# Retention with a gated feed-forward: the order table of the first two batches laid anew, with 25 unread matmuls on zeros among TensorE's first instructions

## The chip, the cores and the metric

One Trainium2 chip, one core of it. The metric is the device time of one execution in microseconds (us), median of several runs. The engines are PE (TensorE), DVE (VectorE), ACT (ScalarE), POOL (GpSimd) and SP, whose queue issues all DMAs of this kernel. Each engine runs its own instructions strictly in program order and waits for others by semaphores.

## The reference

For 8 batches of 8 heads, 576 positions and head width 64:

```python
scores = q @ k.T / sqrt(64)
ret    = scores * D            # D[i, j] = gamma_head ** (i - j) for i >= j, else 0
x      = ret @ v               # heads joined: 576 x 512 per batch
h      = max(x @ w_in, 0)      # 576 x 1024; u = left half, v = right half
v_n    = (v - mean) / sqrt(var + 1e-6)        # over the 512 features
v_s    = w_spatial @ v_n + b_spatial          # mixes the 576 positions
out    = (u * v_s) @ w_out                    # 576 x 512
```

## The kernel before

**Staging.** Matmul operands are float32 split into two rounded parts (`hi`, `lo`), so a product takes three matmuls (hi·hi, hi·lo, lo·hi). The attention runs in chunks of 128 positions (four and a tail of 64 per batch) with a carried state. The weights come from memory as 64-bit floats and are decoded on chip, 128 rows or columns at a time. Batches 0 and 1 use the plain products; batches 2 to 7 use a seven-product scheme on 2 x 2 quarters, whose sums of weight quarters are made once, during the first two batches.

**The order is a table.** Every piece of work is a chain of steps (a Python generator). A table of names says in which order the steps are emitted: each appearance of a name emits the next step of that chain. `ORDER` (656 names) covers batches 0 and 1 and the beginnings of 2 and 3; `STEADY` (249 names) is walked six times, for batches 2 to 7. A step puts instructions on one engine, and the engine keeps the order in which they were emitted. `BANKS` gives, in turn, the PSUM bank (0 to 3) of every step that takes one; a bank is free again when its last reader has run. All instructions are recorded by one helper, so that rows of the profile have one line, L155, and tiles tell them apart.

The names that matter:

- `d.b.c` fetches chunk c of batch b (queries and keys, then the two token-wise parts), `T.b` its tail, `D.k.i` the raw words of weight piece i of kind k (1: right half of `w_in`, 0: left half, 2: `w_out`), `S` the spatial weights, `c.*` constants.
- `w.k.i.xy` decodes a weight piece in seven steps: ACT absolute value; a maximum on engine x (`p` POOL, `v` DVE); three integer steps on DVE, for which a PSUM bank holds the intermediate from the first on until the third has read it; ACT cast to `hi`; on engine y the subtraction that gives `lo`.
- `g.b.c` scores on PE and their mask on DVE; `k`, `q` scale keys and queries; `p.b.c.xy` updates the state (PE, add, decay on x, add on DVE, decay on y); `b.b.c` carries the state and multiplies by the values on PE, then ACT takes `hi` and DVE `lo` of the chunk of x out of PSUM (from batch 2 on ACT alone). `t`, `e` do the same for the tail; the `e` steps leave its `hi` and `lo` in the tile `xt`.
- `v.b.s` is a block of the right half of `h`: four PE steps into a bank, then a chain over ACT and DVE (statistics, normalisation, `hi`, `lo`) that holds the bank to its end; `v.b.4` is the tail block and needs `xt`.
- `U`, `V`, `G`, `P` (batch 0) and `y`, `X` (batch 1) make u, the spatial product, the gate and the split of the gated result; `F.b.t.m` is the output product, copied out by ACT and stored. `F.0.0.1`, the first of them, needs `P.0.0` and `P.0.1`.
- `A.s.n` are the steps that make sums of weight quarters, `R` and `K` the splits and sums of quarters of x for batch 2; `W` are the products of batches 2 to 7. The first, `W.2.0.0.6`, needs both parts of `K.2.6`.

`spin`, which a name `z` calls, is in the kernel before but no table of before has a `z`:

```python
idle = wsp[0][:, 0, :512]              # set to zero by DVE at the start
def spin(name, n):
    ps = bank()
    for i in range(n):
        pe.matmul(ps, idle[:, :P], idle, start=True, stop=True)
```

`idle` is later overwritten by the spatial weights (`s.0`), so `s.0` comes after every `z`.

Of the kernel before, what the change touches and what calls it, by code (L numbers as in the profile page):

```python
# [38 lines left out]


ORDER = """
    D.1.1 w.1.1.vp D.1.0 D.1.3 w.1.1.vp d.0.0 c.k w.1.1.vp D.1.2 c.a w.1.0.vp d.0.0 w.1.3.pp w.1.3.pp w.1.0.vp
# [4 lines left out]
    p.0.1.vv v.0.0 p.0.1.vv k.0.2.p b.0.1 w.0.0.vp b.0.1 q.0.2.p w.0.0.vp g.0.2 b.0.1 w.0.1.pp w.0.1.pp b.0.1
    p.0.2.pp T.0 p.0.1.vv d.0.3 w.0.2.pp p.0.2.pp v.0.0 b.0.1 v.0.0 g.0.2 w.0.1.pp p.0.2.pp w.0.1.pp b.0.2 p.0.2.pp
    b.0.2 c.t w.0.2.pp p.0.2.pp v.0.1 v.0.1 t.0.p t.0.p w.0.1.pp k.0.3.v b.0.2 b.0.2 d.1.0 w.0.2.pp q.0.3.p g.0.3
    t.0.p p.0.3.pp v.0.1 p.0.3.pp v.0.0 v.0.1 p.0.3.pp b.0.2 b.0.2 v.0.2 g.0.3 S d.1.0 p.0.3.pp d.1.1 b.0.3 m  # L50
    w.0.0.vp b.0.3 d.1.1 v.0.1 g.1.0 b.0.3 b.0.3 k.1.0.p w.0.2.pp S v.0.2 v.0.2 d.1.0 v.0.0 D.2.1 q.1.0.p s.0.p
# [34 lines left out]
STEADY = """
    W.a.0.0.6 W.a.0.0.1 W.a.0.0.2.v W.a.0.0.1 W.a.0.0.6 q.b.1.v W.a.0.0.2.v W.a.0.0.5 W.a.0.0.7 W.a.0.0.3
    W.a.0.0.2.v W.a.0.0.7 W.a.0.0.5 W.a.0.0.4 W.a.0.0.5 W.a.0.0.3 W.a.0.0.4 v.a.0.v W.a.0.1.2.p v.a.0.v W.a.0.1.1
    W.a.0.1.7 W.a.0.1.6 k.b.1.p W.a.0.1.1 b.b.0 v.a.2.p W.a.0.1.6 v.a.0.v g.b.1 v.a.0.v T.b v.a.2.p p.b.1.pp b.b.0
    W.a.0.1.2.p b.b.0 g.b.1 d.b.2 b.b.0 W.a.0.1.5 W.a.0.1.2.p W.a.0.1.3 v.a.2.p d.b.2 W.a.0.1.7 p.b.1.pp W.a.0.1.5  # L90
    b.b.0 q.b.2.p d.b.2 W.a.0.1.5 W.a.0.1.4 t.b.p W.a.1.0.1 W.a.0.1.4 p.b.1.pp W.a.0.1.3 k.b.2.p W.a.1.0.6 v.a.3.p
    p.b.1.pp b.b.1 g.b.2 v.a.0.v v.a.1.p v.a.2.p b.b.1 v.a.0.v d.b.3 v.a.3.p W.a.1.0.1 v.a.2.p W.a.1.0.6 p.b.2.vp
    b.b.1 b.b.1 p.b.1.pp g.b.2 d.b.3 W.a.1.0.2.p d.c.0 W.a.1.0.5 b.b.1 p.b.2.vp W.a.1.0.7 k.b.3.p v.a.2.p v.a.4
    W.a.1.0.2.p v.a.4 v.a.1.p W.a.1.0.4 W.a.1.0.2.p W.a.1.0.7 v.a.1.p v.a.3.p v.a.4 d.c.0 p.b.2.vp W.a.1.0.3
    W.a.1.0.5 p.b.2.vp v.a.4 d.b.3 W.a.1.0.5 v.a.4 W.a.1.0.4 W.a.1.1.1 b.b.2 b.b.2 g.b.3 v.a.1.p k.c.0.p W.a.1.0.3
    v.a.4 p.b.3.vp v.a.1.p p.b.2.vp d.c.0 v.a.3.p t.b.p b.b.2 b.b.2 v.a.4 W.a.1.1.6 v.a.1.p v.a.4 v.a.3.p W.a.1.1.1
    q.b.3.p W.a.1.1.2.p p.b.3.vp v.a.4 v.a.3.p W.a.1.1.6 W.a.1.1.7 W.a.1.1.4 v.a.4 W.a.1.1.2.p v.a.4 W.a.1.1.3
    W.a.1.1.7 W.a.1.1.5 W.a.1.1.2.p t.b.p v.a.4 v.a.4 d.c.1 W.a.1.1.5 X.a.1.1 p.b.3.vp W.a.1.1.4 W.a.1.1.5 X.a.0.1
    W.a.1.1.3 X.a.0.1 X.a.0.1 X.a.0.0 b.b.2 p.b.3.vp X.a.0.3 X.a.0.1 b.b.3 X.a.1.1 b.b.3 g.b.3 X.a.1.1 g.c.0 X.a.1.1
    X.a.0.0 p.c.0.pp b.b.3 X.a.0.3 b.b.3 e.b.p X.a.0.3 X.a.0.0 X.a.0.2 X.a.0.3 d.c.1 g.c.0 e.b.p X.a.1.3 e.b.p  # L100
    X.a.1.3 X.a.0.0 R.b.0.0.v X.a.0.2 X.a.0.2 b.b.3 p.c.0.pp p.c.0.pp X.a.1.0 X.a.1.3 X.a.0.2 p.c.0.pp X.a.1.3
    R.b.1.1.p q.c.0.v R.b.0.0.v X.a.1.2 X.a.1.2 d.c.1 K.b.5.pv F.a.0.1 F.a.0.3 X.a.1.0 F.a.0.1 K.b.7.pp F.a.0.2
    X.a.1.0 R.b.1.0.v F.a.0.3 R.b.1.1.p F.a.0.0 X.a.1.2 F.a.0.2 K.b.6.pv F.a.0.2 F.a.0.0 F.a.0.1 p.c.0.pp X.a.1.0
    F.a.0.3 X.a.1.2 F.a.1.1 F.a.1.2 F.a.1.1 F.a.1.3 K.b.6.pv R.b.1.0.v F.a.1.0 F.a.1.2 K.b.5.pv F.a.1.3 K.b.4.pp
    K.b.6.pv F.a.0.0 K.b.7.pp K.b.4.pp F.a.1.0 F.a.1.3 K.b.7.pp F.a.1.2 K.b.4.pp F.a.1.0 F.a.1.1 K.b.5.pv
"""
# [818 lines left out]
```

## Time and profile before

| what | us |
|---|---|
| three runs | 528.2, 528.48, 531.0 (median 528.48) |
| profiled execution, first to last instruction | 526.7 |
| what lies around that span, if that execution was like the median run | 1.8 |

The profile holds no other time for the profiled execution than its span. PE is busy for 95% of it; the granted TensorE clock is 0.996 of full on average. A "busy" PE row is not proof of full speed: rows of neighbouring matmuls overlap, so the distance between starts is the price of one.

### The profile page before, as it was taken

How to read it: one execution, taken by the hardware profiler on the slowest of the kernel's cores; microseconds unless marked ns; L12 is line 12 of the kernel's file. 1: busy time of each engine (PE TensorE's matmuls, PEld its weight loads, DVE VectorE, ACT ScalarE, POOL GpSimd, SP SyncE). 2: the span in 40 equal slices, each digit the busy share in tenths (PEclk: the TensorE clock that was granted, in tenths of full speed). 3: DMA queues.
4: the chain of work that ended last, by engine and by line, in shares of the span. 5: the costliest groups of instructions: out<-in, count | busy, mean ns of one | idle time of the engine just before them, and what ended most of it. 6: DMA issues, size and time to landing. Idle time of an engine off the chain costs nothing.

```text
span 526.7 us, 17043 instructions
## 1 busy us (share of the span) xinstructions
PE 499.3 (95%) x7376; PEld 475.8 (90%) x7376; DVE 353.3 (67%) x803; ACT 222.0 (42%) x502; POOL 236.6 (45%) x216
## 2 busy tenths in 40 slices
PE   0789999999998999999999999999999999999897
PEld 0668998799998999999999999999999999998896
DVE  4998888961536884579654995569745895538640
ACT  4347535562152452444344451445434452444422
POOL 2887769411156720667027740557216750444000
PEclk9999999999998999999999999999999999999999
DMA  8995342403315430163202650155201600020002
GB/s 289 410 321 187 116 157 82 123 18 101 113 59 170 144 105 2 46 197 126 78 2 94 182 168 4 42 157 160 87 2 52 221 11 2 1 91 1 0 1 91
DMA packets 29948, 55.53 MB, mean 105 GB/s; under 512 B 3249, under 2 KB 15793, under 8 KB 29618
## 3 DMA queue, kind: packets, MB, share of 16 engines
q1 hardware_dynamic: 29874, 54.45, 31.4%
q8 instruction: 58, 0.95, 0.7%
q14 instruction: 16, 0.13, 0.1%
HBM read 45.00 MB, written 9.44 MB: 103 GB/s over the span
## 4 chain that ended last, share of the span: by engine, by line
PE 80%; DVE 9%; POOL 3%; issue 3%; DMA 2%; ACT 2%; SPq 0%; ACTq 0%; POOLq 0%; DVEq 0%
PE m L155 69%; PE r L155 11%; DVE u L155 3%; DMA lent_slot<-in_w_in 1%; POOL x L155 1%; DVE sm L155 1%; DMA kn<-in_qkv 1%; POOL u L155 1%; DVE m L155 1%; DVE s L155 1%; DVE vn L155 1%; DVE slot L155 1%; SPq L155 0%; ACT vt L155 0%; DVE dec L155 0%
## 5 line engine op out<-in xcount | busy, mean ns | idle before, releaser
L155 PE MATMUL m<-wsp,vn 128*128 128x288 f32 x768 | 113.5, 297 | 0.4 <-DVE vt L155 0.3
L155 PEld LDWEIGHTS m<-wsp,vn 128*128 128x128 f32 x768 | 105.2, 188 | 2.0 <-DVE vt L155 1.3
L155 PE MATMUL m<-slot,wout 128*128 128x288 f32 x768 | 104.1, 294 | 0.2 <-DVE f L155 0.2
L155 PEld LDWEIGHTS m<-slot,wout 128*128 128x128 f32 x768 | 102.3, 188 | 0.7 <-issue 0.6
L155 PE MATMUL m<-slot,win 128*128 128x288 f32 x480 | 74.2, 299 | 1.8 <-ACT u L155 1.0
L155 DVE TENSOR_TENSOR u<-m,u 128x256 f32<-128x256 f32 (+1 forms) x144 | 59.0, 431 | 24.5 <-ACT u L155 16.5
L155 PEld LDWEIGHTS m<-slot,win 128*128 128x128 f32 x480 | 66.7, 188 | 5.9 <-ACT u L155 2.6
L155 PE MATMUL m<-win,slot 128*128 128x256 f32 (+1 forms) x312 | 56.5, 325 | 2.7 <-issue 1.8
L155 POOL TENSOR_TENSOR x<-x 128x576 f32<-128x576 f32 (+1 forms) x28 | 42.7, 1524 | 21.1 <-DVE slot L155 13.0
L155 PEld LDWEIGHTS m<-win,slot 128*128 128x128 f32 x312 | 45.1, 193 | 7.9 <-DVE u L155 2.1
L155 DVE TENSOR_TENSOR slot<-m,slot 128x288 fp32r<-128x288 f32 x56 | 25.3, 455 | 36.6 <-ACT slot L155 35.8
L155 ACT COPY o<-m 128x288 f32<-128x288 f32 x64 | 25.4, 400 | 55.7 <-PE m L155 52.7
L155 ACT COPY u<-m 128x288 f32<-128x288 f32 (+1 forms) x54 | 20.8, 385 | 57.0 <-PE m L155 42.1
L155 ACT CAST slot<-m 128x288 fp32r<-128x288 f32 x56 | 21.7, 404 | 52.2 <-DVE m L155 52.1
L155 DVE TENSOR_TENSOR slot<-x,slot 128x576 fp32r<-128x576 f32 x24 | 26.9, 1123 | 22.3 <-ACT slot L155 22.3
L155 POOL TENSOR_TENSOR x<-xt 128x256 f32<-128x256 f32 x6 | 4.4, 738 | 81.6 <-DVE xt L155 81.6
L155 PE MATMUL m<-quarter,slot 128*128 128x256 f32 x288 | 39.0, 285 | 2.0 <-ACT o L155 1.3
L155 PEld LDWEIGHTS m<-quarter,slot 128*128 128x128 f32 x288 | 36.2, 191 | 2.8 <-ACT o L155 1.5
L155 DVE SCALAR_TENSOR_TENSOR m<-u,m 128x288 f32<-128x288 f32 x48 | 20.9, 456 | 25.1 <-PE m L155 25.1
L155 ACT CAST slot<-x 128x576 fp32r<-128x576 f32 x42 | 28.4, 680 | 17.0 <-POOL x L155 14.3
L155 POOL TENSOR_SCALAR u<-u 128x512 f32<-128x512 f32 x18 | 26.7, 1500 | 17.6 <-DVE u L155 15.0
L155 POOL TENSOR_TENSOR slot<-x,slot 128x576 fp32r<-128x576 f32 x18 | 26.1, 1465 | 18.2 <-ACT slot L155 18.2
(128 smaller groups left out, 917.2 us busy)
## 6 DMA issues: line engine op xcount, KB each, us to landing
qk<-in_qkv SPq DMA_DIRECT2D x30, 512.0 KB, 4.4
out<-o SPq DMA_DIRECT2D x64, 144.0 KB, 1.8
...
```

The source lines that it names most:

```text
L155: ins = op(*args, **kw)
```

## The change

Only the three strings change. All chains and helpers stay.

- `ORDER` gets 25 new names, each one `z` step: one matmul of a 128 x 128 block of zeros with 512 columns of zeros into a bank that nothing reads.
- The names of `ORDER` come in another order on all engines, the fetches on SP too: the first chunk of attention and its constants are fetched ahead of the first weight pieces, and a second and third chunk between them.
- Some steps change between POOL and DVE (the last letters of a name). 
- `STEADY` has the same 249 names in another text order, and `BANKS` is a new string of 365 digits (340 before).

The diff, cut (the first lines of `ORDER`, its end, the start of `STEADY`):

```diff
 ORDER = """
-    D.1.1 w.1.1.vp D.1.0 D.1.3 w.1.1.vp d.0.0 c.k w.1.1.vp D.1.2 c.a w.1.0.vp d.0.0 w.1.3.pp w.1.3.pp w.1.0.vp
-    w.1.0.vp w.1.0.vp g.0.0 w.1.0.vp d.0.0 w.1.1.vp w.1.0.vp c.q w.1.1.vp w.1.3.pp w.1.2.pp g.0.0 w.1.0.vp w.1.1.vp
-    k.0.0.v p.0.0.vv w.1.3.pp D.0.0 q.0.0.v w.1.3.pp w.1.2.pp p.0.0.vv w.1.2.pp w.1.3.pp c.d b.0.0 b.0.0 w.0.0.vp
...
-    F.1.0.1 R.2.1.0.p R.2.1.1.v R.2.1.1.v F.1.0.2 g.3.0 F.1.0.1 F.1.0.1 A.1.11.v K.2.5.pv K.2.5.pv p.3.0.pp F.1.0.3
-    F.1.0.0 K.2.7.pv K.2.6.pp K.2.4.vv F.1.0.0 F.1.1.0 F.1.1.1 K.2.6.pp F.1.1.2 F.1.1.2 K.2.7.pv K.2.6.pp K.2.4.vv
+    d.0.0 c.d c.k c.a d.0.0 d.0.0 c.q D.1.0 d.0.1 g.0.0 d.0.1 d.0.1 g.0.0 D.1.2 D.1.1 k.0.0.v d.0.2 p.0.0.pp D.1.3
+    q.0.0.v p.0.0.pp b.0.0 p.0.0.pp D.0.0 z.17.1 b.0.0 m w.1.0.vp b.0.0 w.1.0.vp b.0.0 w.1.0.vp d.0.3 p.0.0.pp b.0.0
+    T.0 k.0.1.v g.0.1 p.0.0.pp w.1.0.vp c.t p.0.1.vv q.0.1.p b.0.0 z.22.1 z.0.1 p.0.1.vv z.21.1 w.1.0.vp D.0.1
+    w.1.2.vp b.0.1 g.0.1 z.20.1 b.0.1 z.13.1 p.0.1.vv z.15.1 w.1.2.vp z.24.1 d.1.0 w.1.1.vp b.0.1 p.0.1.vv b.0.1
+    w.1.0.vp p.0.1.vv w.1.1.vp z.4.1 b.0.1 w.1.0.vp w.1.2.vp z.1.1 z.12.1 z.7.1 w.1.1.vp z.19.1 z.23.1 w.1.2.vp
+    z.18.1 z.6.1 z.16.1 w.1.1.vp d.1.0 k.0.2.p z.10.1 z.5.1 g.0.2 w.1.1.vp q.0.2.p b.0.1 p.0.2.pp S w.1.3.vp z.14.1
...
+    R.2.1.0.v d.3.1 F.1.0.3 R.2.1.1.v F.0.1.0 A.1.11.v R.2.0.0.v R.2.1.1.v F.1.0.1 p.3.0.vv R.2.0.0.v K.2.5.vv
+    F.1.1.3 F.1.0.1 F.1.0.3 F.1.0.1 F.1.0.0 K.2.5.vv F.1.0.3 F.1.0.0 F.1.1.1 K.2.5.vv K.2.7.vv p.3.0.vv F.1.1.2
+    K.2.6.vv K.2.6.vv F.1.1.0 F.1.1.1 K.2.6.vv F.1.1.3 K.2.4.vv K.2.7.vv K.2.7.vv F.1.1.0 F.1.1.2 p.3.0.vv K.2.4.vv
...
 STEADY = """
-    W.a.0.0.6 W.a.0.0.1 W.a.0.0.2.v W.a.0.0.1 W.a.0.0.6 q.b.1.v W.a.0.0.2.v W.a.0.0.5 W.a.0.0.7 W.a.0.0.3
+    W.a.0.0.6 k.b.1.p W.a.0.0.1 W.a.0.0.2.v W.a.0.0.1 W.a.0.0.6 W.a.0.0.5 W.a.0.0.2.v T.b W.a.0.0.7 q.b.1.v d.b.2
...
-BANKS = "0123102312103323010313101013013012103002110101302302120132103203201213312013210320213012301321
+BANKS = "0123023012301201212121210210321020010132320320302032032130101131313231313200123132321031213012
...
```

## Rows read from the trace of the kernel before

**Rows 1.** The page: each engine's busy time, share of the span, instructions.

```profile
PE 499.3 (95%) x7376; PEld 475.8 (90%) x7376; DVE 353.3 (67%) x803; ACT 222.0 (42%) x502; POOL 236.6 (45%) x216
```

**Rows 2.** Busy time by stage: stretch, length, engines (instructions), granted clock, DMA share, GB/s.

```profile
0.00:12.00 12.00, 1.13 (x32) 0.94 (x32) 5.27 (x11) 4.54 (x7) 2.06 (x6) 1.00 0.83 280
12.00:44.00 32.00, 25.91 (x626) 20.80 (x627) 29.88 (x59) 14.79 (x33) 27.16 (x27) 1.00 0.91 334
44.00:82.00 38.00, 38.00 (x628) 35.56 (x630) 33.91 (x70) 19.86 (x42) 26.90 (x23) 1.00 0.44 144
82.00:100.00 18.00, 16.68 (x324) 13.87 (x315) 16.77 (x29) 10.55 (x23) 15.18 (x14) 1.00 0.28 83
100.00:160.00 60.00, 60.00 (x822) 58.58 (x821) 30.19 (x66) 23.44 (x56) 14.86 (x15) 1.00 0.29 88
160.00:168.00 8.00, 6.01 (x35) 5.58 (x34) 4.64 (x7) 3.76 (x9) 5.12 (x4) 0.79 0.39 119
168.00:470.00 302.00, 300.47 (x4562) 291.58 (x4561) 203.73 (x489) 126.80 (x292) 136.90 (x125) 1.00 0.28 89
```

**Rows 3.** TensorE's start of the tail block of batch 1, and of the hand-over to batch 2.

```profile
92.99 1.17 PE L155 MATMUL m<-win,xt 128*128 128x512 f32 x4 [0.55 <-DVE xt L155]
...
162.16 0.50 PE L155 MATMUL m<-quarter,slot 128*128 128x256 f32 x2 [1.29 <-ACT o L155]
163.35 0.74 PE L155 MATMUL m<-quarter,slot 128*128 128x256 f32 x4 [0.69 <-POOL slot L155]
```

**Rows 4.** One microsecond after the hand-over, columns as in rows 2.

```profile
164.00:165.00 1.00, 1.00 (x7) 1.00 (x6) 0.99 (x1) 0.15 (x1) 1.00 (x2) 0.50 0.49 173
```

**Rows 5.** The chain that ended last, at the hand-over: start, length, what.

```profile
157.32 1.89 POOL x L155
...
159.28 1.83 POOL x L155
...
161.88 1.42 POOL slot L155
```

**Rows 6.** Timeline of TensorE: distances between starts, and small matmuls early and later.

```profile
19.64 1.13 PE L155 MATMUL r<-vv,kn 64*64 64x64 f32 x32
...
24.23 0.69 PE L155 MATMUL r<-u 64*64 64x64 f32 x32
...
69.25 1.76 PE L155 MATMUL m<-wsp,vn 128*128 128x288 f32 x12
...
71.11 1.76 PE L155 MATMUL m<-wsp,vn 128*128 128x288 f32 x12
```

**Rows 7.** Timeline of ScalarE: first reads of two weight pieces of 0.52 MB.

```profile
5.84 0.66 ACT L155 ACTIVATE lent_vn<-lent_slot 128x512 f32<-128x512 f32 x1 [3.62 <-DMA lent_slot<-in_w_in]
7.60 0.66 ACT L155 ACTIVATE lent_vn<-lent_slot 128x512 f32<-128x512 f32 x1 [1.09 <-DMA lent_slot<-in_w_in]
```

**Rows 8.** Groups by shape, 0 to 100 us: busy, mean ns of one, idle before.

```profile
L155 DVE TENSOR_SCALAR lent_vn<-lent_vn 128x512 f32<-128x512 f32 x2 | 0.9, 426 | 5.7 <-ACT lent_vn L155 5.7
L155 DVE TENSOR_SCALAR m<-f 128x512 int32<-128x512 int32 x8 | 5.5, 682 | 0.0
...
L155 POOL TENSOR_SCALAR f<-f 128x512 f32<-128x512 f32 x6 | 9.4, 1574 | 1.8 <-ACT f L155 1.8
L155 POOL TENSOR_TENSOR x<-win,win 128x512 f32<-128x512 f32 x3 | 3.9, 1291 | 3.5 <-DVE f L155 2.1 <-DVE x L155 1.4
```

**Rows 9.** Timeline: low halves on VectorE; one operation beside POOL's and alone.

```profile
39.12 0.68 DVE L155 TENSOR_TENSOR slot<-r,slot 128x512 fp32r<-128x512 f32 x1
...
68.29 1.30 POOL L155 TENSOR_TENSOR x<-win,win 128x512 f32<-128x512 f32 x1 [2.10 <-DVE f L155]
68.31 1.82 DVE L155 TENSOR_TENSOR x<-win,win 128x512 f32<-128x512 f32 x1
...
92.43 0.41 DVE L155 TENSOR_TENSOR xt<-r,xt 128x256 fp32r<-128x256 f32 x1
...
96.04 0.66 DVE L155 TENSOR_TENSOR x<-win,win 128x512 f32<-128x512 f32 x1
```

More of the change, by code (lines that the diff above doesn't have):

```diff
@@ L47 @@
[L47 to L51, printed above, removed]
@@ new lines @@
+    w.1.3.vp v.0.0 w.0.0.vp w.1.3.vp w.1.2.vp v.0.1 g.0.2 v.0.0 w.0.0.vp p.0.2.pp w.1.3.vp v.0.0 D.0.2 k.0.3.v
+    w.1.3.vp g.0.3 w.0.0.vp d.1.0 w.1.3.vp S w.0.0.vp q.0.3.p S w.0.1.vp t.0.p t.0.p b.0.2 b.0.2 p.0.3.pp t.0.p
+    v.0.1 p.0.3.pp w.0.0.vp v.0.0 b.0.2 g.0.3 p.0.3.pp v.0.1 b.0.2 v.0.0 d.1.1 q.1.0.p w.0.0.vp v.0.1 p.0.3.pp d.1.1
+    v.0.0 k.1.0.p z.2.1 v.0.1 v.0.2 S v.0.0 v.0.1 b.0.3 g.1.0 w.0.1.vp b.0.3 s.0.p b.0.3 v.0.0 b.0.3 v.0.1 s.0.p
+    g.1.0 v.0.2 e.0.p v.0.1 v.0.0 T.1 w.0.0.vp v.0.2 e.0.p w.0.2.pv v.0.0 d.1.1 s.1.p p.1.0.pv w.0.1.vp b.0.3 v.0.4
@@ new lines @@
+    p.1.1.pv v.0.4 v.0.3 w.0.1.vp b.1.1 g.1.2 v.0.4 b.1.1 v.0.3 b.1.1 p.1.2.pv w.0.3.vv d.2.0 v.0.3 b.1.1 D.2.2
+    d.1.3 w.0.2.pv V.0.1 d.2.0 t.1.v w.2.1.vp p.1.1.pv w.2.0.vp w.2.1.vp q.1.3.v V.0.2 g.1.2 V.0.1 b.1.1 b.1.1
+    p.1.2.pv V.0.0 V.0.2 w.2.0.vp p.1.2.pv V.0.0 v.1.0 G.0.1 V.0.0 k.1.3.p w.0.3.vv p.1.2.pv w.2.0.vp b.1.2 g.1.3
+    w.0.3.vv b.1.2 p.1.3.pp G.0.1 t.1.v w.0.3.vv b.1.2 b.1.2 w.2.0.vp w.0.3.vv D.2.3 V.1.0 w.2.1.vp d.2.1 d.2.0
+    w.2.0.vp t.1.v v.1.0 b.1.2 G.0.2 w.2.0.vp V.1.0 q.2.0.v w.2.0.vp w.2.1.vp V.0.3 G.0.2 g.1.3 w.2.3.pp w.2.1.vp
@@ new lines @@
+    V.1.1 w.0.3.vv w.2.3.pp A.0.1.v A.0.5.v p.1.2.pv G.1.1 V.1.1 A.0.0.v v.1.0 b.1.2 V.0.3 p.1.3.pp V.1.3 v.1.0
+    p.1.3.pp A.0.2.v G.1.1 A.0.3 G.0.3 w.2.2.vv A.0.4.v V.1.3 A.0.9.v A.0.6.v V.1.2 A.0.10 G.0.3 P.0.0.p k.2.0.v
+    v.1.0 P.0.0.p w.2.2.vv G.1.3 w.2.2.vv V.1.2 A.0.7 p.1.3.pp P.0.1.v w.2.2.vv b.1.3 A.1.1.v g.2.0 b.1.3 w.2.1.vp
+    b.1.3 g.2.0 b.1.3 q.2.1.p v.1.0 p.2.0.vp b.1.3 T.2 w.2.1.vp v.1.1 d.2.1 b.1.3 d.2.2 G.1.2 w.2.2.vv d.2.1
+    A.0.11.v G.1.3 v.1.3 P.0.1.v v.1.1 A.0.12.v F.0.0.1 A.0.13.v G.1.2 P.1.1.v k.2.1.v v.1.3 F.0.0.1 w.2.3.pp
@@ L104 @@
[L104 to L105 removed]
+    W.a.0.0.6 k.b.1.p W.a.0.0.1 W.a.0.0.2.v W.a.0.0.1 W.a.0.0.6 W.a.0.0.5 W.a.0.0.2.v T.b W.a.0.0.7 q.b.1.v d.b.2
+    W.a.0.0.2.v W.a.0.0.3 d.b.2 W.a.0.0.7 d.b.2 W.a.0.0.5 W.a.0.0.4 W.a.0.0.5 W.a.0.0.3 W.a.0.1.2.p W.a.0.0.4
+    v.a.2.p W.a.0.1.1 v.a.0.v v.a.0.v W.a.0.1.7 W.a.0.1.1 W.a.0.1.6 v.a.0.v W.a.0.1.6 v.a.0.v b.b.0 g.b.1 b.b.0
@@ new lines @@
+    W.a.0.1.2.p W.a.0.1.2.p p.b.1.pp v.a.2.p d.b.3 b.b.0 b.b.0 W.a.0.1.5 d.b.3 q.b.2.p v.a.2.p W.a.0.1.3 g.b.1
+    W.a.0.1.7 W.a.0.1.4 t.b.p p.b.1.pp W.a.0.1.5 b.b.0 v.a.0.v W.a.0.1.5 W.a.1.0.1 p.b.1.pp W.a.0.1.4 W.a.0.1.3
+    k.b.2.p W.a.1.0.6 v.a.3.p p.b.1.pp v.a.2.p v.a.0.v b.b.1 v.a.1.p v.a.3.p g.b.2 b.b.1 W.a.1.0.1 v.a.2.p p.b.2.vp
+    W.a.1.0.6 b.b.1 b.b.1 W.a.1.0.2.p d.c.0 W.a.1.0.5 g.b.2 d.c.0 d.b.3 p.b.1.pp b.b.1 k.b.3.p W.a.1.0.7 p.b.2.vp
+    v.a.2.p d.c.0 v.a.1.p v.a.4 W.a.1.0.2.p v.a.4 W.a.1.0.2.p W.a.1.0.7 v.a.1.p W.a.1.0.4 v.a.3.p v.a.4 p.b.2.vp
@@ new lines @@
+    W.a.1.0.5 W.a.1.0.3 p.b.2.vp W.a.1.0.5 W.a.1.0.4 v.a.1.p v.a.4 W.a.1.1.1 v.a.4 W.a.1.0.3 k.c.0.p p.b.2.vp v.a.4
+    q.b.3.p v.a.3.p b.b.2 g.b.3 b.b.2 v.a.1.p v.a.4 v.a.1.p v.a.3.p p.b.3.vp v.a.4 W.a.1.1.1 t.b.p b.b.2 d.c.1 b.b.2
+    W.a.1.1.6 W.a.1.1.2.p v.a.4 d.c.1 W.a.1.1.7 p.b.3.vp v.a.3.p W.a.1.1.6 v.a.4 W.a.1.1.2.p d.c.1 W.a.1.1.2.p
+    W.a.1.1.4 W.a.1.1.7 v.a.4 W.a.1.1.3 v.a.4 W.a.1.1.5 t.b.p v.a.4 X.a.1.1 W.a.1.1.5 p.b.3.vp W.a.1.1.4 W.a.1.1.5
+    W.a.1.1.3 X.a.0.1 X.a.0.0 X.a.0.1 X.a.0.1 p.b.3.vp X.a.0.1 X.a.1.1 X.a.0.3 b.b.2 g.b.3 b.b.3 b.b.3 X.a.1.1
```

78 lines of the change are left out of this document (28 added, 50 removed).

## The prediction

> **What bounds the kernel now.** First the busy shares [rows 1]: TensorE 95%, VectorE 67%, GpSimd 45%. An average says little here, so next the stages [rows 2]. In the first 44 us TensorE is busy for 1.1 + 25.9 = 27.0 us and VectorE for 35.2; from 12 us on VectorE has hardly a gap (29.9 of 32). From 44 to 82 TensorE is full and VectorE works 33.9 of 38. From 82 to 100 TensorE loses 1.3 and VectorE works 16.8 of 18; from 100 to 160 TensorE is full and VectorE half idle. From 168 to 470 TensorE misses 1.5 of 302. So TensorE sets the time from 44 us on, VectorE is close behind it up to 100, and what can be won lies in the start and between 160 and 168.
>
> There TensorE waits 1.29 + 0.69 us [rows 3], last for the low half of `K.2.6`; the chain is three sums and a subtraction in a row on GpSimd, 1.4 to 1.9 us each [rows 5]. Then the granted clock reads 0.50, the lower of the two levels (1.2 and 2.4 GHz), after this wait [rows 4]; over the 8 us its mean is 0.79 [rows 2], so 8 x 0.21 = 1.7 us are lost. The stall costs about 2.0 + 1.7 = 3.7 us.
>
> **What the batches 2 to 7 get: nothing.** Walking `STEADY` engine by engine, before and after, I find the same sequence on PE, DVE, ACT, POOL and SP; only the interleaving of the text differs. The banks are renamed, nearly everywhere by one permutation, and at the end of a batch a few output products change neighbours. From the first W on the trace should be that of before, shifted. So the whole change is when batch 2 can start and whether it starts at full clock.
>
> **The count of work.** A whole product of twelve 288-column matmuls and two more takes 71.11 - 69.25 = 1.86 us from start to start [rows 6], 0.133 each, 0.136 with the turn from one kind to the next; 512 columns by the same excess over their columns 0.229, 32 small ones 0.50 (estimates, from the same row). In these prices TensorE has 132.7 us of work before the first W in both tables. It ends that work at 162.16 - 1.29 = 160.9 [rows 3], so by then it has lost 28.2; with the stall and the slow clock 31.9. This is the number to beat.
>
> **Moved between engines.** In `ORDER` 30 operations leave GpSimd for VectorE: 7 sums of weight quarters, 6 maxima, 5 decays, 3 sums of x, 3 tail copies, 2 + 2 scalings, 2 splits. GpSimd pays 1.29 to 1.57 us for the common ones [rows 8], VectorE 0.43 for a maximum [rows 8] and 0.66 for a sum alone [rows 9], together some 17 us more for VectorE. After 100 us that is covered (it is idle half the time), before it is not.
>
> Two points of VectorE's queue show it, counted in those prices (integer steps 0.68, masks and low halves 0.68, adds 0.41). Up to the low half of batch 0's last chunk it has 32.3 us of work before the change and 30.8 after; up to the low half of batch 1's tail 76.8 before and 85.3 after. In the trace these end at 39.8 and 92.8 [rows 9]: a lag (time minus work) of 7.5, then 16.0. TensorE's tail block of batch 1 waits for the second [rows 3].
>
> **The start.** The first fetch, 0.52 MB, is there at 5.8, a second one 1.76 us later [rows 7]; from 12 to 44 us the queues move 334 GB/s at a share of 0.91 [rows 2], 0.37 MB/us when full. Attention's first fetch now takes the first place, so (estimates) mask and keys land at 6.5 and 7.2, values at 8.0, the first weight piece at 9.8, the second chunk at 11.2 to 12.6. Further back on SP the spatial weights stand behind the integer steps that free their place (about 21.5), and hold the fetches after them till then; the first of these is wanted past 36. Step by step: scores 5.8 to 6.9, mask to 7.6, keys to 8.3, update to 9.4, carried and values to 11.5, low half at 14.2, when VectorE has done 5.4 us of work. From about 12 on something is always ready, and the hand count has 39.9 for the last chunk's low half: a lag of 9.1. The earlier attention thus gives VectorE no lead; its decoding starts later, and the stretch ends at the same time (39.8 before).
>
> **The spins.** 25 matmuls of 0.23 us, or 0.38 at the early rate (by 1.13 against 0.69 for the same matmuls [rows 6]), are 6 to 9 us. TensorE has 16.4 us of real work up to 38.5 by the same count, so 22 us of waiting hide them; without that cover they would cost all of it. Each takes a bank: it waits for that bank's last reader, and the next integer step of a decode on this bank waits for it. At worst the second piece's first integer step is held 0.9 us behind the values of chunk 1, and behind it on VectorE the rest of that decode; also the update of chunk 2 stands behind eleven spins. Price on the lag 0 to 2.5, taken 0, since the count of before has the same kind of gaps.
>
> Small matmuls run at 1.13 us for 32 up to some 20 us and at 0.69 from 24 us on [rows 6], while the granted clock is reported as 1.00 throughout [rows 2]. The Trainium skill (TensorE: Matmul & The Clock Gate, Why this matters for your kernels) wants TensorE kept busy without a break to get the full clock; by it alone the spins would save some ten such groups at 0.44 each, about 4 us more. By the rows they save nothing, since VectorE, not TensorE, ends that stretch.
>
> **From 40 to 100 us.** VectorE's lag grew by 8.5 in before; 4.9 of it was idle time, waiting for a TensorE that was full [rows 2], 3.6 the lengthening of operations that meet GpSimd: the same sum takes 1.82 beside GpSimd and 0.66 alone [rows 9]. After, 27 such operations stand in this stretch instead of 17, and GpSimd's work falls from 38.9 in 53 us to 22.7 in 54.5. So 3.6 x 27/17 x 0.417/0.734 = 3.2. Bounds: 0, and 8.5 once more. I take 3.2 with no idle time, as VectorE would now be the one waited for. Then the tail's low half ends at 85.3 + 9.1 + 3.2 = 97.6. TensorE has 67.0 us of work ahead of the tail block: it has lost 30.6 there. On the way it meets VectorE again and again (banks that the gates and v chains hold, the splits for `F.0.0.1`), each a little less late.
>
> **From 100 to the hand-over.** No further wait on VectorE comes out of the count: the last v block of batch 1 wants its bank at about 112 and TensorE is there at 113. `R` and `K` now run on VectorE: behind the last chunk's values TensorE has eight output products, 13.0 us; the copy out is done 3.3 us after the values, then come on VectorE splits, a decay, sums and subtractions of 0.74 (0.66 x 576/512, the price of [rows 9] by size) with casts between, and the low half of `K.2.6` is ready 11.7 after the values. So no stall and no fall of the clock.
>
> **Sum.** Loss up to batch 2: 30.6 against 31.9, minus 1.3. Span 526.7 - 1.3 = 525.4, and with the 1.8 around it 527.2, against the median of 528.5. Below 0.5% (2.6 us) a measurement of this kernel can't be told from no change.
>
> **Rivals.**
> - *A, likeliest:* the 3.7 of the hand-over are won, and VectorE's longer queue takes most of it back: 527.2, with growths of the lag from 2 to 7 us 526 to 531. For it: VectorE's near-full rows up to 100.
> - *B, VectorE keeps pace:* the lag does not grow, since a quieter GpSimd lengthens nothing. TensorE has lost 27.4 at the tail block (94.4 - 67.0); 4.5 less than before, 524.0. For it: in 12 to 44 us, with GpSimd nearly full, the lag did not grow in before. Against it: the 1.82 of [rows 9].
> - *C, slower:* the lag grows by the 8.5 of before although VectorE is the later one (chains over ACT, TensorE's turns, the spins' banks). Tail at 102.9, loss 35.9, plus 4.0: 532.5. It decides where the lag at the tail passes 13.6; from 16.2 on it is slower by over 0.5%.
> - *D, the hand-over stalls again:* `K` still late, clock falls; A plus 3.7: 530.9.
>
> **Chances.** A 0.43, B 0.31, C 0.18, D 0.08. Faster by over 0.5%: B and a little of A, 0.32. Within: most of A and half of D, 0.44. Slower: C and the rest, 0.24. The range for 8 in 10 runs from 523.0 (B with a lag 1 us smaller) to 532.0 (nearly C); A's own is 526 to 531.
>
> **What would show it.** Per-engine order from the first W on as before, and the span from there shorter only by the hand-over. VectorE's tail low half of batch 1 at 97 to 99 (B: 94 to 95, C: 102 or later); the first values at about 11.5; TensorE waiting for VectorE between 60 and 100 in small pieces; no 0.50 clock around batch 2's start and no wait for the low half of `K.2.6`. I am wrong if TensorE is full from 45 to 100 (then B), if the first 12 us bring VectorE a lead, or if a stall shows up between 100 and 160.

## The result, and the profile after

The changed kernel takes 534.52 us (median of four runs, 532.38 to 535.99), the kernel before 528.53 beside it. The ratio is 1.0103, 95% interval 1.007 to 1.0136: slower by 1%, 6 us, and outside the range. The profiled execution took 534.0 us with a span of 531.9, against 526.7 before.

The stages of the changed kernel, in the stretches of [rows 2] (columns as there):

```profile
0.00:12.00 12.00, 3.78 (x78) 2.85 (x81) 2.38 (x6) 2.62 (x5) 1.62 (x7) 1.00 0.82 234
12.00:44.00 32.00, 28.34 (x597) 22.17 (x598) 25.82 (x56) 14.43 (x29) 19.04 (x19) 1.00 0.82 308
44.00:82.00 38.00, 37.58 (x587) 34.66 (x586) 36.08 (x81) 21.60 (x46) 17.59 (x18) 1.00 0.54 173
82.00:100.00 18.00, 17.38 (x305) 15.47 (x308) 17.08 (x30) 7.30 (x16) 5.08 (x4) 1.00 0.28 83
100.00:160.00 60.00, 59.69 (x867) 58.02 (x857) 36.31 (x84) 27.23 (x65) 9.19 (x8) 1.00 0.29 89
160.00:168.00 8.00, 8.00 (x67) 8.00 (x66) 6.78 (x13) 3.97 (x9) 0.00 (x0) 1.00 0.30 102
168.00:470.00 302.00, 296.74 (x4522) 286.48 (x4521) 197.79 (x488) 123.58 (x286) 135.33 (x124) 1.00 0.28 89
```

From 160 to 168 TensorE is full at a granted clock of 1.00, where [rows 2] had 6.01 of 8 us at 0.79. The hand-over did what it was to do; GpSimd has nothing there any more. The loss is in the last line: from 168 to 470 TensorE misses 5.3 us of 302, before it missed 1.5. The stretch for which the prediction had forecast nothing at all is where the time went.

TensorE at the hand-over of the changed kernel, in answer to [rows 3] (start, length, what, idle before):

```profile
152.78 11.50 PE L157 MATMUL m<-slot,wout 128*128 128x288 f32 x86
164.12 0.87 PE L157 MATMUL m<-quarter,slot 128*128 128x256 f32 x6
```

No idle time stands ahead of the first W. By ScalarE's copy of the product `W.2.0.1.1` the changed kernel is 0.66 us ahead; the row after the change, then the row before it:

```profile
170.64 0.37 ACT L157 COPY u<-m 128x256 f32<-128x256 f32 x1 [3.87 <-PE m L157]
```

```profile
171.30 0.37 ACT L155 COPY u<-m 128x256 f32<-128x256 f32 x1 [4.27 <-PE m L155]
```

What TensorE waits for in the changed kernel, the longest groups (total, times, longest):

```profile
PE r L157 <- issue: 5.4, 3, 3.4
PE r L157 <- DMA qk<-in_qkv: 5.2, 1, 5.2
PE m L157 <- ACT o L157: 2.9, 6, 0.5
```

Two of these lines stand out. **Six waits of 0.5 us for `o`,** ScalarE's copy of an output tile, one per steady batch; the kernel before has one such wait, the 1.29 of [rows 3]. **Three idle times marked "issue"**, in which TensorE waited for nothing that the trace shows. These are not new: the kernel before has three too, 2.7 us in all (1.83 at 37.84, 0.37 and 0.48 later), where the changed kernel has 5.4 and a fourth of 0.23. The timeline of the changed kernel at the longest "issue" idle and at the first wait for `o`:

```profile
30.52 0.52 PE L157 MATMUL r<-lent_wout 64*64 64x64 f32 x23
34.47 0.38 PE L157 MATMUL r<-lent_wout 64*64 64x64 f32 x9 [3.43 <-issue]
...
212.82 0.56 PE L157 MATMUL m<-slot,wout 128*128 128x288 f32 x3
213.87 2.38 PE L157 MATMUL m<-slot,wout 128*128 128x288 f32 x16 [0.49 <-ACT o L157]
```

The upper pair breaks off in the middle of 32 alike matmuls, of which 23 have already run on the same tiles. The lower wait stands between two output products: `F.2.0.3` has been given bank 2, which `F.2.0.1` directly before it has just filled, and must wait for the copy out. The start times of ScalarE's copy of `F.b.0.3`, from the two traces:

| batch | 2 | 3 | 4 | 5 | 6 | 7 |
|---|---|---|---|---|---|---|
| before | 215.69 | 276.45 | 337.57 | 398.80 | 459.39 | 513.43 |
| after | 215.75 | 277.27 | 340.06 | 401.57 | 463.79 | 518.57 |
| difference | +0.06 | +0.82 | +2.49 | +2.77 | +4.40 | +5.14 |

Four of the five steps between neighbours are 0.74 to 1.67 (the two larger ones hold an "issue" idle besides, near 328 and 428 us) and one is 0.28, where the kernel before has an "issue" idle of 0.48. At the place itself, ScalarE copies `F.2.0.1` and `F.2.0.3` 2.34 us apart (213.41, 215.75), before 1.58 (214.11, 215.69). So a wait that the trace shows as 0.49 costs 0.74 to 0.76; what the other quarter of a microsecond is, no row shows.

### The profile page after: what moved, and what is told of

Same layout as the page of the kernel before. It is cut to its first block, busy times and chain, and to the rows that moved or that the text cites. A ratio compares the mean times of both kernels' runs of the same rounds, so it can differ in the third digit from the quotient of the medians.

```text
span 531.9 us, 17064 instructions
## 1 busy us (share of the span) xinstructions
PE 507.4 (95%) x7401; PEld 480.9 (90%) x7401; DVE 352.4 (66%) x833; ACT 222.0 (42%) x502; POOL 197.5 (37%) x186
## 4 chain that ended last, share of the span: by engine, by line
PE 72%; DVE 13%; DMA 4%; issue 4%; ACT 3%; POOL 3%; SPq 1%; DVEq 0%; ACTq 0%; POOLq 0%
PE m L157 62%; PE r L157 10%; DVE u L157 4%; DMA vv<-in_qkv 2%; DVE sm L157 2%; POOL u L157 1%; DVE s L157 1%; DVE vn L157 1%; DMA kn<-in_qkv 1%; DMA raw<-in_w_out 1%; ACT vt L157 1%; DVE f L157 1%; SPq L157 1%; DVE x L157 1%; DVE m L157 1%
## 5 line engine op out<-in xcount | busy, mean ns | idle before, releaser
L157 PE MATMUL m<-slot,wout 128*128 128x288 f32 x768 | 105.2, 295 | 2.9 <-ACT o L157 2.9
L157 PE MATMUL m<-win,slot 128*128 128x256 f32 (+1 forms) x312 | 54.2, 318 | 0.2
L157 DVE TENSOR_TENSOR slot<-x,slot 128x576 fp32r<-128x576 f32 x27 | 22.9, 847 | 24.6 <-ACT slot L157 24.5
L157 POOL TENSOR_TENSOR x<-x 128x576 f32<-128x576 f32 x20 | 30.1, 1505 | 14.6 <-DVE slot L157 13.8
L157 PE MATMUL m<-slot,quarter 128*128 128x288 f32 x216 | 34.1, 297 | 0.0
L157 PEld LDWEIGHTS m<-slot,quarter 128*128 128x128 f32 x216 | 30.5, 188 | 0.9
```

The source lines that it names most:

```text
L157: ins = op(*args, **kw)
```

## The experiments

The theories. **1, banks:** the six waits make 6 x 0.73 = 4.4 us. **2 to 4, the spins**, which the prediction had as free: they cost by what they put ahead of other work; or by the "issue" idle times, either because these come from full DMA engines (3) or because 25 more matmuls move all later work against fixed places of TensorE's instruction stream (4). Rivals: the head of the table, or the new interleaving of `STEADY`, makes the loss. Ratios are to the kernel before, measured beside each, with 95% intervals.

### Which bank: e1, e2, e4, then e5 and e6

**e1.** The digits that `F.2.0.1` to `F.2.1.0` take in batch 2 (other batches alike):

```diff
-22312031
+23212031
```

> The changed kernel with one edit: in the six steady batches the bank of the output product F.b.0.3 is exchanged with that of F.b.0.2, so that it no longer takes the bank of F.b.0.1, which TensorE does directly before it. Theory 1 (the banks): TensorE's six waits for ScalarE's copy of an output tile (3 us idle in all) go away, and with them a growth of about 0.73 us at each of the six places; the time falls by 4.4 us, from 534.5 to about 530, a ratio of about 1.003 to the kernel before. Rival 1 (the changed head or the changed order of the steady step makes the loss, and the waits only fill a gap that comes anyway): the time stays within 1 us of 534.5.

Measured: 540.79, ratio 1.0241 (1.0211 to 1.0271). This is no test of the theory. In the new text order `F.a.0.3` is named before the last stage of `X.a.1.3`, so the product overwrites a tile whose lower half has not been taken; part of the output is another one for that, and VectorE waits for the product instead (a line of its waits in e1: total, times, longest):

```profile
DVE slot L157 <- PE m L157: 23.4, 6, 4.9
```

That may be why the changed table had used the other bank at all. **e2** has the same fault from the other side (`F.b.0.3` overwrites `F.b.0.1` before its copy):

```diff
-10103210
+11031230
```

> The kernel before with one edit: in the six steady batches F.b.0.3 takes the bank of F.b.0.1, as the changed kernel has it, and the products behind it take the banks that this frees. Nothing else of the change is in it. Theory 1 (the banks): 6 x 0.73 = 4.4 us slower, about 533, a ratio of 1.008. Rival 1 (the waits cost nothing by themselves): within 1 us of 528.5.

Measured: 535.3, ratio 1.0133 (1.0104 to 1.0161); nothing follows from it. **e4** is e1 without the 25 `z` names, with e1's overwritten tiles:

> The changed kernel with the exchange of banks of e1 and without the 25 spins (their names and their bank digits are taken out; they are matmuls on zeros that nobody reads). Theory 1 (the spins gain nothing, and cost VectorE 1.5 us where it waits for a spin's bank at 19.75 us): same as e1 or up to 1.5 us faster, 528.5 to 530. Rival 2 (the spins hold TensorE's clock up through the first 40 us and pay for themselves): slower than e1 by 2 us or more, with a lower granted clock in the first 40 us.

Measured: 534.66, ratio 1.0125 (1.01 to 1.015). Alone it says little, but against e1, which has the same fault, it is 6.1 us faster: the spins cost something.

**e5** names the product behind the stage that frees the bank:

```diff
-F.a.0.1 F.a.0.3 p.c.0.pp X.a.1.3
+F.a.0.1 p.c.0.pp X.a.1.3 F.a.0.3
-22312031
+23212031
```

> The changed kernel with F.b.0.3 off the bank of F.b.0.1, done so that the output stays as it was: in the steady step F.a.0.3 is named behind X.a.1.3's last stage, which frees bank 3 of batch 2 (and what answers to it in the other batches), and takes that bank; F.a.0.2 takes the bank that F.a.0.3 had. No engine's own order changes. Theory 1 (the banks): TensorE's six waits for ScalarE's copy (0.49 us each in the row, about 0.73 us each in the comparison of the two traces) go, 4.4 us faster than the changed kernel's 534.5: about 530, ratio 1.003. Rival 1 (the loss is elsewhere): within 1 us of 534.5.

**e6** is the bad bank alone, in the kernel before:

```diff
-F.a.0.1 F.a.0.3 X.a.1.0 F.a.0.1
+F.a.0.1 X.a.1.0 F.a.0.1 F.a.0.3
-10103210
+11013210
```

> The kernel before with the bank order of the change alone: F.b.0.3 is named behind F.b.0.1's copy and takes F.b.0.1's bank, F.b.0.2 takes the one that F.b.0.3 had, F.b.0.0 that of F.b.0.1. No engine's own order changes. Theory 1 (the banks): 6 x 0.73 = 4.4 us slower than 528.5, about 533, ratio 1.008. Rival 1: within 1 us of 528.5.

Measured: e5 529.8, ratio 1.0017 (0.9995 to 1.004); e6 532.84, ratio 1.0074 (1.0048 to 1.01). That is 534.5 - 529.8 = 4.7 faster and 532.84 - 528.88 = 4.0 slower (2.5 to 5.3 by e6's interval), theory 1's 4.4 from both sides. In e5 the wait for `o` is gone from TensorE's list and the two copies are 1.59 us apart again; in e6 the list has six more such waits, each with 0.49 in TensorE's rows. ScalarE's copies of `F.2.0.1` and `F.2.0.3` in e5, then in e6:

```profile
212.24 0.40 ACT L157 COPY o<-m 128x288 f32<-128x288 f32 x1 [2.05 <-PE m L157]
...
213.83 0.40 ACT L157 COPY o<-m 128x288 f32<-128x288 f32 x1 [0.25 <-PE m L157]
```

```profile
216.41 0.40 ACT L155 COPY o<-m 128x288 f32<-128x288 f32 x1 [2.05 <-PE m L155]
...
218.75 0.40 ACT L155 COPY o<-m 128x288 f32<-128x288 f32 x1 [1.00 <-PE m L155]
```

### The hand-over alone: e3

The new letters (each name wherever it stands in `ORDER`):

```diff
-R.2.0.0.p R.2.1.0.p e.2.p K.2.5.pv K.2.7.pv K.2.6.pp
+R.2.0.0.v R.2.1.0.v e.2.v K.2.5.vv K.2.7.vv K.2.6.vv
```

> The kernel before with one part of the change: the hand-over into batch 2 (the three steps K.2.5, K.2.6 and K.2.7, two of the R.2 steps and the lower half of the tails' copy e.2) goes from GpSimd to VectorE by the letters of the order table; head, banks and steady step are as before. As the prediction priced it: the stall of 2.0 us ahead of W.2 and the 1.7 us of halved clock behind it go, 3.7 us faster, about 524.8, ratio 0.993. Rival: VectorE still works off its lag there, so that its lower halves come later than GpSimd's did; the stall stays or grows, 528 to 531.

Measured: 527.04, ratio 0.9977 (0.9962 to 0.9993): 1.2 us (0.4 to 2.0) of the 3.7. TensorE at the hand-over in e3, and the granted clock behind it:

```profile
163.54 0.50 PE L155 MATMUL m<-quarter,slot 128*128 128x256 f32 x2 [0.49 <-ACT o L155]
164.45 0.74 PE L155 MATMUL m<-quarter,slot 128*128 128x256 f32 x4 [0.41 <-DVE slot L155]
```

```profile
164.00:166.00 2.00, 1.59 (x13) 1.54 (x13) 1.73 (x3) 1.54 (x6) 0.00 (x0) 1.00 0.10 35
166.00:168.00 2.00, 2.00 (x19) 2.00 (x18) 1.36 (x3) 0.74 (x2) 0.00 (x0) 1.00 0.85 271
```

Against the trace of before the clock's part comes in full (1.00 against the 0.50 of [rows 4]); of the stall 0.9 of 2.0 stays. In this execution the work ahead of the hand-over ended 2.2 us later than in the trace of before (163.05 against 160.87): the "issue" idle near 38 us was 2.11 instead of 1.83, and the granted clock behind it reads 0.50 from 38.0 to 41.4 us, 1.00 before. By the copy of `W.2.0.1.1` e3 is 0.39 ahead (170.91 against 171.30), so the hand-over itself won 2.6 in this pair of traces. That the medians differ by only 1.2 has a reason on record: in 11 of the 17 executions of the kernel before beside e3 the granted clock was 0.998 or more on average, too much for a fall like that of [rows 4] (0.996 in the profiled one). So most of these had no 1.7 us of slow clock to win back; the prediction took it from the one that was profiled. Why VectorE's chain is no faster in the table of before was not looked into.

### The spins: e7, e8, e9

**e7** is e5 with the 25 `z` names and their digits taken out.

> The changed kernel, banks as in e5_banks_mended, without the 25 spins. In e4's trace TensorE passed its 475th matmul without the 3.43 us of idle that the changed kernel has behind it, and the chain of batch 0's last chunk was 4 us earlier at 41 us. Theory 2 (the spins cost by what they put ahead of TensorE's own work): the 4 us last up to batch 2, 4 us faster than e5: about 526, ratio 0.995. Rival 2 (the lead is used up by VectorE and GpSimd before batch 2): within 1 us of e5. By the clock rival (the spins hold the clock up): slower than e5.

Measured: 524.59, ratio 0.9911 (0.988 to 0.9941), 5.2 below e5, and faster than both kernels of the case. Measured again (e16) it was 524.01, ratio 0.9912 (0.9886 to 0.9938):

> The kernel of e7 unchanged, beside the shifted ones on the same chip: 524.6 again, within 1 us.

TensorE's idle times marked "issue" in the profiled executions: e5 3.44 at 32.37, 0.97 at 325.35, 0.78 at 423.30; e7 0.49 at 67.05, 1.48 at 143.74; e16 none. e7 and e16 are the same kernel, so one trace does not tell how long such an idle is in another execution. ScalarE around the first, in e5 and then in e16 (the same two steps, the split of chunk 2's x and the first step of batch 0's first v block):

```profile
29.31 0.59 ACT L157 CAST slot<-r 128x512 fp32r<-128x512 f32 x1 [0.93 <-DVE att L157]
35.73 0.58 ACT L157 ACTIVATE m<-m 128x512 f32<-128x512 f32 x1 [5.83 <-PE m L157]
```

```profile
32.22 0.59 ACT L154 CAST slot<-r 128x512 fp32r<-128x512 f32 x1 [2.71 <-DVE att L154]
33.73 0.58 ACT L154 ACTIVATE m<-m 128x512 f32<-128x512 f32 x1 [0.92 <-PE m L154]
```

Here one sees both sides of the spins. With them attention is 2.9 us ahead at 29 us. That lead is TensorE's pace: the twelve matmuls of 512 columns ahead of it took 2.96 us with the spins and 4.90 without, and 32 small ones took 0.65 at 17.74 us with them, 1.08 at 17.57 without. The granted clock reads 1.00 there in both traces, so this shows in the times of the rows alone. The row of e5, then that of e16:

```profile
24.08 2.96 PE L157 MATMUL m<-win,slot 128*128 128x512 f32 x12
```

```profile
25.17 4.90 PE L154 MATMUL m<-win,slot 128*128 128x512 f32 x12 [0.22 <-ACT r L154]
```

At 36 us the lead has become 2.0 behind, 4.9 lost. The idle of 3.44 is the larger part of it; with it came a fall of the granted clock in e5, from 32.0 to 35.4 us:

```profile
32.00:35.40 3.40, 3.03 (x15) 2.43 (x16) 2.34 (x5) 0.00 (x0) 1.83 (x3) 0.50 0.86 307
```

The two later idle times add to it. The spans are 526.0 and 522.5, so this pair shows 3.5 of the 5.2; e5's profiled execution was its fastest (528.16). Eight of the traces have such a fall within 1.6 us of the end of an early idle of 2.11 to 3.44 us; the changed kernel's own (3.43) has none. Over all executions the granted clock was 0.9953 on average in e5 and 0.9994 in e7, so at most 526 x 0.0041 = 2.2 us of the 5.2 are the clock's (an estimate).

**e8** and **e9** move fetches back, to see whether full DMA engines hold TensorE up. e8: the five `S` names behind the second `d.1.1`. e9: the third `d.1.0`, `D.0.2` and two `d.1.1` behind `T.1`.

> The changed kernel with e5's banks, with spins, and with the five fetch steps of the spatial weights (1.4 MB, in the changed kernel issued at 20.9, 26.5 and 30.3 us) moved behind the second fetch of chunk 1.1 on SyncE, so that they start after 29 us. The DMA engines' share was 1.00 to 1.05 up to 35 us in the changed kernel, and TensorE's 3.43 us of idle ended at 34.47, when that share fell. Theory 3 (the idle is late delivery of TensorE's instructions behind the full DMA engines): the idle behind the 475th matmul shrinks to 1 us or less, and the time falls 1 to 3 us below e5. Rival 3 (the place in the instruction stream alone makes the idle, whatever the DMA engines do): it stays at about 3.4 us, and the time is e5's, or above it where the later weights are waited for.

> The kernel of e5 (changed, banks mended, spins kept) with 1.5 MB of fetches (the last part of chunk 1.0, the weights D.0.2, the first two parts of chunk 1.1) moved behind the fetch of batch 1's tails, which SyncE issues at 40.2 us; in e8 the moved fetches had started at 26.7 us and the DMA engines stayed full. Its whole time says little, because weight halving and chunk 1.1 then wait. What counts is TensorE's idle behind its 475th matmul. Theory 3 (it is late delivery of instructions behind the full DMA engines): with some 3.7 us less to move, the idle shrinks from 3.4 to 2 us or less. Rival 3 (only the place in the stream matters): 3.1 to 3.5 us again.

Measured: e8 530.11, ratio 1.0024 (1.0003 to 1.0045), idle 3.16. It decides nothing: the fetches only changed places, and from 30 to 35 us the share was still 0.94. e9, a single run, 536.64, idle 3.16 again, while the DMA engines ran empty (the third line is the first microsecond of the idle):

```profile
29.40 0.52 PE L156 MATMUL r<-lent_wout 64*64 64x64 f32 x23
33.08 0.38 PE L156 MATMUL r<-lent_wout 64*64 64x64 f32 x9 [3.16 <-issue]
```

```profile
25.00:30.00 5.00, 4.92 (x132) 3.92 (x131) 4.93 (x9) 2.08 (x4) 4.14 (x5) 1.00 1.04 404
30.00:35.00 5.00, 1.92 (x15) 1.54 (x16) 1.63 (x4) 0.59 (x1) 2.79 (x4) 0.93 0.26 69
...
30.00:31.00 1.00, 0.00 (x0) 0.00 (x0) 0.20 (x1) 0.59 (x1) 1.00 (x1) 1.00 0.74 185
```

Theory 3's "2 us or less" fell: the share during the idle is far below e5's, the idle 3.2 instead of 3.4. But the engines were full (1.04) until the idle began at 29.92, so this does not rule out a delivery that was asked for earlier and held up then; the end of the section on e10 to e15 comes back to it.

### The place in the instruction stream: e10 to e15

Count the matmuls that TensorE has done when an "issue" idle comes: busy time from the start to the idle, instructions in brackets. The kernel before, then the changed one (twice), then e5 (twice):

```profile
0.00:37.80 37.80, 20.88 (x603) 16.88 (x603) 30.37 (x57) 14.61 (x30) 24.36 (x28) 1.00 0.93 340
```

```profile
0.00:34.40 34.40, 22.59 (x475) 17.37 (x475) 19.64 (x39) 10.10 (x19) 14.77 (x19) 1.00 0.96 345
...
0.00:327.90 327.90, 312.59 (x5062) 293.29 (x5063) 234.17 (x542) 142.59 (x319) 124.22 (x121) 1.00 0.40 132
```

```profile
0.00:32.30 32.30, 20.91 (x475) 16.34 (x475) 19.48 (x39) 10.41 (x19) 14.85 (x19) 1.00 0.95 344
...
0.00:325.30 325.30, 311.41 (x5062) 293.06 (x5063) 236.10 (x542) 142.76 (x319) 124.34 (x121) 0.99 0.40 133
```

603 = 475 + 128. Whatever the work and the time, the early idle comes behind nearly the same count modulo 128: 91 at 347, 475 and 603, 92 at 348 (e11), 90 at 602 (e4) and 730 (e15). Later the remainder drifts down slowly (86 at 1110 and 81 at 2129 in e7, 70 at 5062 and 65 at 6465 in the changed kernel, 61 at 6461 in e3). The traces explain the drift: they also record TensorE's semaphore and drain instructions, 69 in the changed kernel and 77 in the one before. Count each matmul as two instructions, since its weight load has a record of its own, and each of these as one. Then all 50 "issue" idle times of the 18 traces, 0.18 to 3.44 us long, stand behind a count that leaves 192 or 193 when divided by 256. So the 25 spins shift all later work by 25 against these places. The Trainium skill (Runtime: NRT & Kernel Launch, Instruction fetch mechanics) says that an engine's instruction memory is refilled in blocks of 256 instructions, which agrees with this count, and that crossing from one to the next is mostly hidden: each kernel here passes some 58 such places, and 0 to 5 of them show an idle, but the 3.43 is not hidden.

**e10**, **e12**, **e11**: short spins (64 columns for 512) in front of everything in e7, in place in e5, in front in the kernel before.

```diff
-            pe.matmul(ps, idle[:, :P], idle, start=True, stop=True)
+            pe.matmul(ps[:, :D], idle[:, :P], idle[:, :D], start=True, stop=True)
```

> The kernel of e7 (changed, banks mended, no spins) with 25 matmuls of 64 columns on zeros put in front of everything, where TensorE waits 4.5 us for its first fetch anyway. They take next to no time and no bank that is wanted, but every later instruction of TensorE stands 25 matmuls further back, as in e5. Theory 4 (the spins' price is the shift of TensorE's instruction stream, whose idle times stood at the same place modulo 128 matmuls in every kernel so far): the idle of about 3.4 us behind matmul 475 comes back, with about 1 us each near 325 and 423 us, and the time is e5's, 528 to 530. Rival 4 (the price is the spins' time and the banks they take between the real work): e7's 524.6.

> The kernel of e5 with the 25 spins where they are and on the banks they have, but 64 columns wide instead of 512: the same number of instructions and the same waits for banks, an eighth of the streamed columns. Theory 4 (the shift): e5's 529 to 530, with 3 us or more of idle behind matmul 475. Rival 4 (the spins' own time): 1 to 4 us faster than e5, towards e7's 524.6.

> The kernel before with the same 25 short matmuls on zeros in front of everything, and nothing else changed. Theory 4: TensorE's idle of 1.8 to 2.4 us, which stood behind its 603rd matmul in the kernel before and in e3, stands behind its 603rd again, now counted with the 25, that is 25 matmuls earlier in the work; the stalls marked issue near 313 and 372 us move or go; the time moves by up to 2 us, either way. Rival 4: no idle moves, and the time is 528 to 529.

Measured: e10 529.71, ratio 1.0014 (0.9993 to 1.0034); e12 529.18, 1.0011 (0.9989 to 1.0034); e11 529.94, 1.0015 (0.9999 to 1.0032). e12 is e5's time with an eighth of the streamed columns, so it isn't the spins' own time. It is not e5 in all else: its idle behind 475 is 2.13, below the 3 that was expected, and TensorE's pace rises later (the twelve matmuls of 512 columns took 4.12 us, 2.96 in e5), two differences that go against each other. e10 has the idle times of e5 again, smaller in the first place:

```profile
32.96 0.52 PE L154 MATMUL r<-lent_wout 64*64 64x64 f32 x22
34.24 0.44 PE L154 MATMUL r<-lent_wout 64*64 64x64 f32 x10 [0.76 <-issue]
...
326.41 0.44 PE L154 MATMUL r<-att,tail 64*64 64x64 f32 x11 [0.81 <-issue]
...
424.67 0.52 PE L154 MATMUL r<-at,vv 64*64 64x64 f32 x21 [1.05 <-issue]
```

but its short matmuls took 1.50 to 7.04 us, past the first fetch, so part of its time is a late start. In e11 the idle behind 603 came 0.64 long, with one of 0.81 behind 348 and one of 0.77 behind 475 before it; those near 313 and 372 us are gone, others stand at 328.11 and 426.11 us, and the time hardly moved.

**e13, e14, e15**: e7 with a smaller matmul in front, written 128, 25 and 64 times.

```diff
+            r, c = slice(0, D), slice(i % 2 * D, i % 2 * D + D)
-            pe.matmul(ps, idle[:, :P], idle, start=True, stop=True)
+            pe.matmul(ps[c, :16], idle[r, c].bitcast(F32), idle[r, :16].bitcast(F32), start=True, stop=True)
```

> The kernel of e7 with 128 small matmuls (64 rows, 64 columns of weights, 16 columns streamed) on zeros in front of everything, in TensorE's first wait of 4.5 us. Every later instruction of TensorE stands 128 matmuls further back: the same place modulo 128 as in e7. Theory 4 (what counts is the place of the work modulo 128 matmuls): e7's time again, 524 to 526.5, with no idle of issue near 325 and 423 us. Rival 4 (more instructions cost, wherever they stand, or the start gets late): 529 or more.

> The same with 25 such matmuls: e10 without its late start. Theory 4: e5's places modulo 128, so idle of issue behind matmul 475 and about 1 us each near 325 and 423 us, 527.5 to 530. Rival 4: as e7, 524.6.

> The same with 64 such matmuls, half a period. Theory 4: places that neither e5 nor e7 had; idle of issue at other points of the work, none behind the 475th matmul's work of e5, and a time of its own between 523 and 531. Rival 4: as e7, 524.6.

The sizes came out otherwise than meant: each is two matmuls in the trace (50 records for 25). So e14 shifts by 50, e15 by 128, a whole period, and e13 by 256, two periods; and in e15 and e13 they delay the first scores to 8.14 and 14.97 us (4.55 in e7). Measured:

| kernel | shift | us | ratio (95%) | "issue" idle times behind 160 us |
|---|---|---|---|---|
| e7, e16 | 0 | 524.59, 524.01 | 0.9911 (0.988 to 0.9941), 0.9912 (0.9886 to 0.9938) | none |
| e15 | 128 | 526.34 | 0.9955 (0.9933 to 0.9977) | none |
| e13 | 256 | 533.59 | 1.0091 (1.0067 to 1.0115) | none |
| e14 | 50 | 527.28 | 0.9966 (0.995 to 0.9983) | 1.11 at 265.95 |
| e5 | 25 | 529.8 | 1.0017 (0.9995 to 1.004) | 0.97 at 325.35, 0.78 at 423.30 |
| e10 | 25 | 529.71 | 1.0014 (0.9993 to 1.0034) | 0.38 at 310.36, 0.81 at 326.41, 1.05 at 424.67 |

By time alone e13 went against its expectation: it starts 10 us late and keeps 9.3 of that. e15, meant as half a period, tested a whole one. In both no idle stands behind 160 us, as in e7 and e16: whole periods leave the later work where it was, a part of a period brings idle times at new work. Sharpest is one of before 160 us, which e13 shares with e7 (e16 does not have it): e7's at 143.74 stands behind matmul 2129, e13's at 151.38 behind 2385 = 2129 + 256, both three matmuls before the end of the same product. In e13, then in e7 (the idle, and what TensorE had done by then):

```profile
151.38 0.33 PE L154 MATMUL r<-at,vv 64*64 64x64 f32 x3 [1.19 <-issue]
...
0.00:151.30 151.30, 140.34 (x2385) 129.34 (x2386) 109.02 (x235) 66.10 (x143) 51.93 (x53) 1.00 0.47 159
```

```profile
143.74 0.33 PE L154 MATMUL r<-at,vv 64*64 64x64 f32 x3 [1.48 <-issue]
...
0.00:143.70 143.70, 127.07 (x2129) 116.05 (x2130) 109.22 (x235) 66.33 (x143) 51.84 (x53) 1.00 0.49 168
```

And e14's 50 small matmuls, which end before the first fetch lands, cost 527.28 - 524.3 = 3.0 us (524.3 is the middle of e7 and e16) by the shift and what follows from it. Its idle times:

```profile
33.54 0.27 PE L154 MATMUL r<-at,u 64*64 64x64 f32 x2 [2.25 <-issue]
...
265.95 1.33 PE L154 MATMUL m<-wsp,vn 128*128 128x288 f32 x8 [1.11 <-issue]
```

Theory 4 stands for the place. Idle times of over 0.4 us stand in or directly behind a run of 64x64 matmuls, of which some 30 pass in half a microsecond. All traces together say a little more. Of the places that TensorE reached within 2.5 us of the one before, 22 of 52 show an idle, of those it reached after more than 5 us, 6 of 811. The time from one place to the next with the idle added is 2.3 to 4.2 us where the DMA engines' share was under 0.15 on the way, 5.3 to 11.2 where it was 1.0 or more. That is what a delivery of instructions would look like which full DMA engines slow down, theory 3 and theory 4 together; it is a comparison of unlike places, not an experiment, and what sets the length of an idle stays open.

## Why the prediction was wrong, point by point

Two rows of VectorE in the changed kernel, for the third point: the low halves of batch 0's last chunk and of batch 1's tail.

```profile
43.58 0.69 DVE L157 TENSOR_TENSOR slot<-r,slot 128x512 fp32r<-128x512 f32 x1
...
96.03 0.42 DVE L157 TENSOR_TENSOR xt<-r,xt 128x256 fp32r<-128x256 f32 x1
```

- **"What the batches 2 to 7 get: nothing" failed.** The order on each engine is indeed the same, but the sentence passed over its own remark, "at the end of a batch a few output products change neighbours". That is the first of two failed steps: priced at 0, measured 0.73 x 6 = 4.4 in the traces, 4.7 (e5) and 4.0 (e6) in the times. None of the rivals had it; C ends on this side, but by a lag of VectorE that did not come. The new interleaving of the text isn't innocent: a tile's release is counted in the text's order, so moving `X.a.1.3`'s last stage back behind `F.a.0.3` takes away the bank that the product had before.
- **The spins at 0 to 2.5 us, taken as 0, failed too,** and not by the mechanism priced there. VectorE did wait for a bank that spins take (1.48 us at 21.22 in the changed kernel), but in e5, with the spins, attention was still 2.9 us ahead of e16 at 29 us. They cost 529.8 - 524.3 = 5.5 us by the shift of TensorE's stream, the fall of the clock behind the long idle included. "By the rows they save nothing" failed as well: TensorE came to the quick pace earlier. The remark on the Trainium skill (TensorE: Matmul & The Clock Gate, Why this matters for your kernels), some 4 us won, is borne out in part by the lead of 2.9 us at 29 us; that lead didn't live to 36.
- **The loss up to batch 2: -1.3 forecast, -0.66 measured.** The total was near by luck, its parts weren't. The last chunk's low half ended at 44.27, not 39.9: a lag of 13.5 instead of 9.1, of which 3.43 is TensorE's idle. From there to 96.45 (97.6 forecast) the lag fell to 11.2 instead of growing by 3.2, the third term that was wrong: VectorE keeps pace, rival B's mechanism, and the sum `x<-win,win` took 0.68 in the row at 96.69, against 1.82 beside GpSimd in [rows 9]. The two errors cancelled. Without the spins the tail's low half ended at 93.8 (e16) and 94.6 (e7); B had said 94 to 95.
- **The hand-over:** no stall and no fall of the clock in the changed kernel, as forecast. Alone in the table of before (e3) it gives 1.2 of the 3.7: the stall goes only in part, and the 1.7 for the clock was a price that 11 of the 17 executions of the kernel before beside it did not pay.
- **The balance.** By the ratios, of 528.5 us: the table without spins and with mended banks -4.7 (0.991; its 524.3 is about rival B's 524.0), with the spins +0.9 (1.0017), with the banks as changed +5.4 (1.0103). So the spins take 5.6 and the banks 4.5, for which e6 gives 3.9 (1.0074) in a kernel that has nothing else of the change. What of the -4.7 is the new head and what the hand-over, no run separates.
